# Dilated sliding attention and a soft mixture of experts on one core: 128-key tiles with halo products, four heads abreast, logits on column groups, the last weights in halves

## The chip, the cores and the metric

The kernel runs on one core of a Trainium2 chip. A core has a matrix engine (TensorE, PE in the profile, with its weight loads listed apart as PEld), a vector engine (DVE), a scalar engine (ACT), a general engine (POOL, which here only issues DMAs) and a queue engine (SP); 16 DMA engines move data between main memory and the on-chip memory (SBUF). Matrix products land in a small accumulator memory, PSUM, of eight banks of 512 fp32 values per partition. Each engine runs its own instructions in order and waits for others by semaphores. The metric is the device time of one execution in microseconds; the time of a kernel is the median of its runs.

## The reference

There are two stages. For 8 batches, 8 heads, 576 positions and a head width of 64:

```
scores = q @ k.T / 8
plain heads (0-3): keep 0 <= i-j < 32
dilated heads (4-7): keep 0 <= i-j < 128 and (i-j) % 4 == 0
attn = softmax(scores) @ v
x = attn with the heads side by side      # 4608 rows of 512
```

Then a soft mixture of 8 experts with 4 slots each, over all 4608 rows:

```
logits = x @ phi                          # 4608 x 32
d = softmax of logits over the rows;  slot_input = d.T @ x
slot_out[e] = relu(slot_input[e] @ w1[e]) @ w2[e]
out = softmax of logits over the slots @ slot_out
```

All inputs are fp32 in main memory (q, k and v are 9.4 MB each, w1 and w2 16.8 MB each), and so is the output (9.4 MB).

## The kernel before

Every load is a POOL DMA that turns fp32 into fp16 on the way. The program is written as a loop over b (10 passes: 8 batches and two to drain), each with six steps kt; the framework that builds the kernel then orders each engine's instructions by their dependencies, so the instructions of neighbouring steps are interleaved on an engine.

**Attention of one batch.** q and k of a batch arrive as `raw` tiles (L145), and DVE transposes them in 32x32 blocks: the plain heads in one instruction each (`qk_plain`, L200), the dilated heads in two parts (`qk_dil`, L209), sorted by position modulo 4 so that a dilated head becomes four plain windows of 144 positions, called residues. A head occupies 32 partitions, its width of 64 being two halves `tt`. The plain heads work in six tiles of 96 queries against 128 keys, the 32 keys ahead of a tile being part of it; this is why v is copied in a shifted form (`shift_v_plain` L184, `shift_v_left` L180). The dilated heads work in four residues of 128 queries, and 16 queries are left over in each. `emit_scores` (L238) computes a step: two heads at a time (`pair`), each on its own 32 rows of the array and in its own PSUM bank. ACT takes the exponent (L251), DVE multiplies by the mask (L256). `emit_av` multiplies by v with a column of ones (so the row sums come along), eleven products a batch (L273, L291, L304), and DVE divides (L314 reciprocal, L315 multiply). v takes three DMAs a batch: the plain heads (L157), the dilated heads (`vsa`, L163, spread by ACT at L174) and the left-over (`vsb`, L166). v tiles exist three times, raw tiles twice.

**Slots.** One batch later x is transposed by PE (L330, L342) and copied by ACT (L335, L345, L348), the logits are computed with phi repeated four times so that all 128 partitions hold the same 32 rows four times (L360, two instructions groups of 288 columns each), and ACT writes exp(logits) to `ET` (L363). Two batches later ET is transposed (`ep`, L374 to L384), masked to `er` (L391) and used for the slot sums `u` (L405), which DVE adds to `UT` (L411).

**Experts and output.** After the loop: slot inputs (L543 to L549), `hps` against w1 (L563), row sums `rs` (L572), relu (L580, L581), transposes (L584), `so` against w2 (L597), copies to `so_sb` (L604, L605), then 36 blocks of 128 output rows: one matmul (L613), one scaled copy on ACT or DVE (L616, L618), one POOL DMA (L621).

**Order of loads.** POOL issues q, k, one w1 (two in b = 3) at step kt 1 of each pass and v at kt 3, two batches ahead; in passes 6 and 7 it issues the last w1 and the eight w2, some into q/k and v tiles that have come free (L193). The lines in the code that say so:

```
for _ in range((1, 1, 1, 2, 1, 1)[b]):
    load_w1(next_w1.pop(0))
...
if b + 2 < B:
    load_v(b + 2)
```

Of the kernel before, what the change touches and what calls it, by code (L numbers as in the profile page):

```python
# [15 lines left out]
B = 8  # L16
H = 8
S = 576
# [14 lines left out]
QT = 96  # L33
NT = S // QT
SUB = S // DIL
VW = 72
LEFT = SUB - 128
NLEFT = 5 * LEFT
WP = NT // 2 * QT
NE = NT + DIL + 1  # L40
NFIN = N_ROWS // 128


def make_masks():

    a = np.arange(128)[:, None]
    i = np.arange(QT)[None, :]
    rel = 32 + i - a
    plain = (rel >= 0) & (rel < WINDOW)
    c = np.arange(LEFT)[None, :]  # L50
    rel = 32 + c - a
    left = (rel >= 0) & (rel < WINDOW) & (a < 48)
    i = np.arange(128)[None, :]
    rel = i - a
    dil = (rel >= 0) & (rel < WINDOW)
    m = [plain] * 3 + [left] * 5 + [dil] * 4
    ok = ((np.arange(128)[:, None] % 32) < LEFT) & np.ones((1, N_SLOTS), bool)
    m.append(ok)
    return np.ascontiguousarray(np.concatenate(m, axis=1).astype(np.float16))
# [3 lines left out]
def kernel(  # L63
# [12 lines left out]
    mask_np = make_masks()  # L76
    masks_dram = nc.inline_tensor(mask_np, name="masks_d")
    ident_dram = nc.inline_tensor(np.eye(128, dtype=np.float16), name="ident_d")
# [3 lines left out]
    masks = consts.tile([128, mask_np.shape[1]], FP16, name="masks")  # L82
    mask_p = masks[:, 0 : WP + NLEFT]
    mask_d = masks[:, WP + NLEFT : WP + NLEFT + 512]
    ident = consts.tile([128, 128], FP16, name="ident")
# [3 lines left out]
    emask = consts.tile([128, NE, N_SLOTS], FP16, name="emask")  # L89
    ET = consts.tile([128, N_ROWS + 64], FP16, name="ET")  # L90
# [3 lines left out]
    rrow = consts.tile([128, NFIN], FP32, name="rrow")  # L94
    so_sb = consts.tile([128, DMODEL], FP16, name="so_sb")
# [4 lines left out]
    w2t = {e: w2a_pool.tile([128, 8, DMODEL], FP16, name=f"w2_{e}", tag=f"w2_{e}") for e in range(2)}  # L100
# [4 lines left out]
    QK_SLAB, V_SLAB = 2 * (32 + S + S + 80 + S + S + 16), 4096  # L105
    kTp, kTd, qTp, qTd, vP, vD, vL = [], [], [], [], [], [], []
    for i in range(2):
        slab = fix.tile([128, QK_SLAB], FP16, name=f"qk{i}", tag=f"qk{i}")
        o = 0
        for dst, n in ((kTp, 32 + S), (kTd, S + 80), (qTp, S), (qTd, S + 16)):  # L110
            dst.append(slab[:, o : o + 2 * n].rearrange("p (s t) -> p s t", t=2))
            o += 2 * n
    for i in range(NV):
        slab = fix.tile([128, V_SLAB], FP16, name=f"v{i}", tag=f"v{i}")
        o = 0
        for dst, n in ((vP, NT), (vD, DIL), (vL, DIL)):
            dst.append(slab[:, o : o + n * 4 * VW].rearrange("p (h n d) -> p h n d", h=4, n=n))
            o += n * 4 * VW

# [6 lines left out]
    p_pool = tc.alloc_tile_pool(name="pp", bufs=4)  # L126
# [5 lines left out]
    psum_s = tc.alloc_tile_pool(name="psum_s", bufs=2, space=bass.MemoryType.PSUM)  # L132
# [22 lines left out]
    def load_v(b):  # L155
        vt = vP[b % NV]
        nc.gpsimd.dma_start(  # L157
            out=vt[32:128, :, :, 0:D], in_=v[b, 0:4].rearrange("h (t a) d -> a (h t) d", t=NT)
        )
        sa = vs_pool.tile([128, 4, DIL * D], FP16, name=f"vsa_{b}", tag="vsa")  # L160
        sb = vs_pool.tile([128, 4, DIL * D], FP16, name=f"vsb_{b}", tag="vsb")
        vstage[b] = (sa, sb)
        nc.gpsimd.dma_start(  # L163
            out=sa, in_=v[b, 4:8, 0:512, :].rearrange("h (a r) d -> a h (r d)", r=DIL)
        )
        nc.gpsimd.dma_start(  # L166
            out=sb[32 : 32 + LEFT],
            in_=v[b, 4:8, 512:576, :].rearrange("h (a r) d -> a h (r d)", r=DIL),
        )

    def spread_v_dil(b):
        sa, sb = vstage.pop(b)
        for st, dst, p0, n in ((sa, vD[b % NV], 0, 128), (sb, vL[b % NV], 32, LEFT)):
            nc.scalar.copy(  # L174
                out=dst[p0 : p0 + n, :, :, 0:D],
                in_=st[p0 : p0 + n].rearrange("a h (r d) -> a h r d", r=DIL),
            )

    def shift_v_left(b):
        nc.vector.tensor_copy(out=vL[b % NV][0:32, :, :, 0:D], in_=vD[b % NV][96:128, :, :, 0:D])  # L180

    def shift_v_plain(b):
        vt = vP[b % NV]
        nc.vector.tensor_copy(out=vt[0:32, :, 1:NT, 0:D], in_=vt[96:128, :, 0 : NT - 1, 0:D])  # L184

# [3 lines left out]
    def load_w2(e, pieces=1):  # L189
        n = 8 // pieces  # L190
        src = moe_w2[e].rearrange("(c p) f -> p c f", p=128)
        for i in range(pieces):
            nc.gpsimd.dma_start(out=w2t[e][:, n * i : n * i + n, :], in_=src[:, n * i : n * i + n, :])  # L193


    def qk_plain(ti, b):
        src = raw[(ti, b)][:, 0, :].bitcast(U32).rearrange("p (j m) -> p j m", m=32)
        t = qTp[b % 2] if ti == 0 else kTp[b % 2][:, 32 : 32 + S, :]
# [15 lines left out]
    def emit_scores(b, kt):  # L214
        kp, kd, qp, qd = kTp[b % 2], kTd[b % 2], qTp[b % 2], qTd[b % 2]
        sps = psum_s.tile([128, 2, 512], FP32, name=f"s_{b}_{kt}", tag="s")
        jobs = []
        if kt < 4:
            pair, half = kt % 2, kt // 2
            for i in range(3):  # L220
                t = 3 * half + i
                jobs.append((kp, QT * t, qp, QT * t, QT * i, QT))
            n = WP
            if half == 1:
                for r in range(DIL):
                    w = LEFT if r < 3 else 2 * LEFT
                    jobs.append((kd, SUB * r + 96, qd, SUB * r + 128, WP + LEFT * r, w))
                n = WP + NLEFT
        else:
            pair = kt - 4  # L230
            for r in range(DIL):
                jobs.append((kd, SUB * r, qd, SUB * r, 128 * r, 128))
            n = 512
        for kt_, k0, qt_, q0, c0, w in jobs:
            for tt in range(2):
                for hh in range(2):
                    p0 = 32 * (2 * pair + hh)
                    nc.tensor.matmul(  # L238
                        sps[:, hh, c0 : c0 + w],
                        kt_[p0 : p0 + 32, k0 : k0 + 128, tt],  # L240
                        qt_[p0 : p0 + 32, q0 : q0 + w, tt],
# [3 lines left out]
        return sps, n  # L245

    def emit_exp(b, kt, sps, n):
        tag, w = (("pa", WP), ("pb", WP + NLEFT), ("pd", 512))[kt // 2]
        pt = p_pool.tile([128, 2, w], FP16, name=f"{tag}_{b}_{kt}", tag=tag)
        ptile[(b, kt)] = (pt, n)  # L250
        nc.scalar.activation(out=pt[:, :, 0:n], in_=sps[:, :, 0:n], func=AF.Exp, scale=SCALE)  # L251

    def emit_mask(b, kt):
        pt, n = ptile[(b, kt)]
        m = (mask_p if kt < 4 else mask_d)[:, 0:n]
        nc.vector.tensor_tensor(  # L256
            out=pt[:, :, 0:n],
            in0=pt[:, :, 0:n],
            in1=m[:, None, :].broadcast_to([128, 2, n]),
# [4 lines left out]
    xp_t, xd_t = {}, {}  # L264

    def emit_av(b, tl):
        o = psum_o.tile([128, 4, D + 1], FP32, name=f"o_{b}_{tl}", tag="o")
        if tl < NT:
            half, i = divmod(tl, 3)
            nq = QT if (half == 0 and i == 2) else 128  # L270
            for h in range(4):
                pt, _ = ptile[(b, 2 * half + h // 2)]
                nc.tensor.matmul(  # L273
                    o[0:nq, h, :],
                    pt[:, h % 2, QT * i : QT * i + nq],
                    vP[b % NV][:, h, tl, 0 : D + 1],
                    start=(h == 0),
                    stop=(h == 3),
                    skip_group_check=True,
                )  # L280
            if b not in xp_t:
                xp_t[b] = x_pool.tile([128, NT, 4 * D], FP16, name=f"xp_{b}", tag="xp")
            dst, nq = xp_t[b][0:QT, tl, :], QT
        else:
            r = tl - NT
            if b not in xd_t:
                xd_t[b] = x_pool.tile([128, DIL + 1, 4 * D], FP16, name=f"xd_{b}", tag="xd")
            if r < DIL:
                for h in range(4):
                    pt, _ = ptile[(b, 4 + h // 2)]  # L290
                    nc.tensor.matmul(  # L291
                        o[:, h, :],
                        pt[:, h % 2, 128 * r : 128 * r + 128],
                        vD[b % NV][:, h, r, 0 : D + 1],
                        start=(h == 0),
                        stop=(h == 3),
                        skip_group_check=True,
                    )
            else:
                for r in range(DIL):  # L300
                    for h in range(4):
                        pt, _ = ptile[(b, 2 + h // 2)]
                        c0 = WP + LEFT * r
                        nc.tensor.matmul(  # L304
                            o[32 * r : 32 * r + 32, h, :],
                            pt[0:48, h % 2, c0 : c0 + 32],
# [350 lines left out]
```

## Time and profile before

| what | us |
|---|---|
| median of 3 runs | 203.83 |
| the runs | 202.67 to 204.26 |
| span of the profiled execution | 200.8 |
| PE, DVE, ACT, POOL busy | 146.6, 132.3, 100.6, 66.9 |
| PE weight loads busy | 91.8 |

Main memory is read for 62.20 MB and written for 9.44 MB. The span runs from the first to the last instruction of the profiled execution; the time of a run is longer by what lies around it, 3.0 us by the median of the runs (the page doesn't give the profiled execution's own time). In the page's second part the span is cut into 40 slices of 5.0 us, and a digit is the busy share in tenths. PEclk is the clock of PE that the records of the profile give, in tenths; GB/s counts what the DMAs wrote. A matmul's row in the timeline has its start, its duration (which includes the time through the array, so that consecutive matmuls overlap), the engine, the line, output and inputs, shapes and a count. A weight shape of 32*128 means 32 rows of the array and 128 output rows. A wait's row has the engine and line that waited, what it waited for, and the sum, count and longest of the waits in us. In the chain of waits a row has start, duration, engine, tile and line.

### The profile page before, as it was taken

How to read it: one execution, taken by the hardware profiler on the slowest of the kernel's cores; microseconds unless marked ns; L12 is line 12 of the kernel's file. 1: busy time of each engine (PE TensorE's matmuls, PEld its weight loads, DVE VectorE, ACT ScalarE, POOL GpSimd, SP SyncE). 2: the span in 40 equal slices, each digit the busy share in tenths (PEclk: the TensorE clock that was granted, in tenths of full speed). 3: DMA queues.
4: the chain of work that ended last, by engine and by line, in shares of the span. 5: the costliest groups of instructions: out<-in, count | busy, mean ns of one | idle time of the engine just before them, and what ended most of it. 6: DMA issues, size and time to landing. Idle time of an engine off the chain costs nothing.

```text
span 200.8 us, 5070 instructions
## 1 busy us (share of the span) xinstructions
PE 146.6 (73%) x2128; PEld 91.8 (46%) x2128; DVE 132.3 (66%) x354; ACT 100.6 (50%) x150; POOL 66.9 (33%) x102
## 2 busy tenths in 40 slices
PE   0126369399889989979799998998886869758600
PEld 0115256158647746646465675675655344211000
DVE  3688697678896998597779678986632120755520
ACT  2037448384872963595386675565433020655510
POOL 7736224215215403501750003055000000598850
PEclk9999999999999999999999999955555599995555
DMA  6999999999999999999999999999999400499994
GB/s 128 182 191 192 205 211 189 209 212 187 211 210 188 214 210 203 196 212 194 204 210 189 208 207 208 207 208 208 207 207 205 70 0 0 127 407 407 410 407 124
DMA packets 46422, 40.99 MB, mean 204 GB/s; under 512 B 20672, under 2 KB 33600, under 8 KB 46400
## 3 DMA queue, kind: packets, MB, share of 16 engines
q0 software_dynamic: 46112, 40.41, 117.0%
q8 instruction: 16, 0.26, 0.5%
q1 hardware_dynamic: 288, 0.27, 0.4%
q14 instruction: 6, 0.05, 0.1%
HBM read 62.20 MB, written 9.44 MB: 357 GB/s over the span
## 4 chain that ended last, share of the span: by engine, by line
PE 41%; DMA 23%; ACT 10%; issue 10%; DVE 7%; POOL 6%; POOLq 0%; ACTq 0%
DMA v_93<-in_v_dram 10%; DMA vsa_1638<-in_v_dram 8%; DMA vsa_148<-in_v_dram 5%; PE so L597 3%; POOL out_dram L621 3%; ACT ET L363 3%; PE hps L563 3%; DVE qk_89 L200 1%; ACT v_92 L174 1%; PE lg_0_977 L360 1%; PE s_4_1993 L238 1%; PE lg_0_1329 L360 1%; PE lg_0_2031 L360 1%; PE lg_0_626 L360 1%; POOL raw_0_121 L150 1%
## 5 line engine op out<-in xcount | busy, mean ns | idle before, releaser
L238 PEld LDWEIGHTS <-qk_89 32*128 32x128 f16 x448 | 14.1, 116 | 22.3 <-DVE qk_89 L200 10.5
L238 PEld LDWEIGHTS <-qk_90 32*128 32x128 f16 x448 | 14.4, 113 | 10.3 <-issue 5.1
L621 POOL DMA_DIRECT2D out_dram<-ot_3191 x1 | 0.6, 561 | 33.4 <-ACT ot_3191 L616 33.4
L360 PEld LDWEIGHTS <-phi_61 128*128 128x128 f16 x64 | 7.6, 128 | 8.1 <-issue 3.5
L613 PEld LDWEIGHTS <-ET 128*128 128x128 f16 x36 | 3.6, 99 | 14.3 <-issue 13.0
L238 PE MATMUL s_0_178<-qk_89 32*128 32x96 f16 x12 | 0.7, 270 | 9.1 <-DVE qk_89 L200 9.1
L193 POOL DMA_DIRECT2D w_5_2337<-in_moe_w_dram x1 | 0.9, 873 | 18.0 <-PE o_0_2311 L273 18.0
L580 ACT ACTIVATE h_sb<-hps 128x512 f16<-128x512 f32 x1 | 0.6, 598 | 9.8 <-PE hps L563 9.8
L605 DVE CAST so_sb<-so 128x256 f16<-128x256 f32 x1 | 0.4, 425 | 6.8 <-ACT so_sb L604 6.8
L581 DVE TENSOR_SCALAR h_sb<-hps 128x512 f16<-128x512 f32 x1 | 0.7, 692 | 6.3 <-ACT h_sb L580 6.3
L251 ACT ACTIVATE pa_0_191<-s_0_178 128x576 f16<-128x576 f32 x1 | 0.7, 651 | 7.8 <-PE s_0_178 L238 7.8
L374 PEld LDWEIGHTS <-ET 32*128 32x128 f16 x48 | 1.9, 99 | 5.5 <-ACT ET L363 5.5
L238 PE MATMUL s_2_214<-qk_89 32*128 32x96 f16 (+2 forms) x28 | 1.1, 215 | 4.3 <-DVE qk_89 L209 3.7
L405 PEld LDWEIGHTS <-ones 96*128 96x128 f16 x48 | 4.0, 103 | 0.0
L563 PEld LDWEIGHTS <-siTm 128*32 128x32 f16 x64 | 2.1, 128 | 4.1 <-issue 2.5
L563 PE MATMUL hps<-w_0_76,siTm 128*32 128x512 f16 x8 | 3.2, 548 | 1.0 <-DVE siTm L549 1.0
L193 POOL DMA_DIRECT2D w_7_2689<-in_moe_w_dram x4 | 2.8, 707 | 3.1 <-PE o_0_2663 L273 2.9
L157 POOL DMA_DIRECT2D v_92<-in_v_dram x3 | 3.6, 1195 | 0.7 <-DMA raw_0_121<-in_q_dram 0.7
L200 DVE STREAM_TRANSPOSE qk_89<-raw_0_121 128x576 uint32<-128x576 uint32 x1 | 1.3, 1256 | 3.9 <-DMA raw_0_121<-in_q_dram 3.9
L184 DVE COPY v_93<-v_93 32x1280 f16<-32x1280 f16 x2 | 1.0, 484 | 4.2 <-DMA v_93<-in_v_dram 4.2
L157 POOL DMA_DIRECT2D v_91<-in_v_dram x3 | 3.6, 1209 | 0.0
L391 DVE TENSOR_TENSOR er_2948<-ep_2933,emask 128x352 f16<-128x352 f16 x1 | 0.3, 342 | 4.9 <-PE ep_2933 L384 4.9
(1047 smaller groups left out, 614.0 us busy)
## 6 DMA issues: line engine op xcount, KB each, us to landing
w_0_76<-in_moe_w_dram POOLq DMA_DIRECT2D x1, 1024.0 KB, 18.6
w_1_77<-in_moe_w_dram POOLq DMA_DIRECT2D x1, 1024.0 KB, 18.6
w_2_78<-in_moe_w_dram POOLq DMA_DIRECT2D x1, 1024.0 KB, 14.8
w_3_79<-in_moe_w_dram POOLq DMA_DIRECT2D x1, 1024.0 KB, 13.5
w_4_80<-in_moe_w_dram POOLq DMA_DIRECT2D x1, 1024.0 KB, 17.7
w_5_81<-in_moe_w_dram POOLq DMA_DIRECT2D x1, 1024.0 KB, 16.0
w_6_82<-in_moe_w_dram POOLq DMA_DIRECT2D x1, 1024.0 KB, 13.4
w_7_83<-in_moe_w_dram POOLq DMA_DIRECT2D x1, 1024.0 KB, 18.5
```

The source lines that it names most:

```text
L150: nc.gpsimd.dma_start(out=t[:, g, :], in_=ten[b, 4 * g : 4 * g + 4].rearrange("h (p j) d -> (h p) (j d)", j=PJ),)
L157: nc.gpsimd.dma_start(out=vt[32:128, :, :, 0:D], in_=v[b, 0:4].rearrange("h (t a) d -> a (h t) d", t=NT))
L193: nc.gpsimd.dma_start(out=w2t[e][:, n * i : n * i + n, :], in_=src[:, n * i : n * i + n, :])
L200: nc.vector.transpose(out=dst, in_=src)
L238: nc.tensor.matmul(sps[:, hh, c0 : c0 + w], kt_[p0 : p0 + 32, k0 : k0 + 128, tt], qt_[p0 : p0 + 32, q0 : q0 + w, tt], start=(tt == 0), sto ...
L360: nc.tensor.matmul(lp, phi4[:, kc].rearrange("p c s -> p (c s)"), rhs, start=(kc == 0), stop=(kc == 3))
L363: nc.scalar.activation(out=ET[:, b * S : b * S + S].rearrange("p (i r) -> p r i", r=DIL)[:, 2 * rp : 2 * rp + 2, :], in_=lp, func=AF.Exp, ...
L405: nc.tensor.matmul(up[:, c, :], l, rr, start=(i == 0), stop=(i == len(jobs) - 1), skip_group_check=True)
L563: nc.tensor.matmul(hps[32 * j : 32 * j + 32, fc, :], siTm[:, dc, e, :], w1t[e][:, dc, 512 * fc : 512 * fc + 512], start=(g == 0 and dc == ...
L597: nc.tensor.matmul(so[32 * j : 32 * j + 32, :], hTm[g][:, c, 32 * j : 32 * j + 32], w2t[4 * g + j][:, c, :], start=(g == 0 and c == 0), st ...
L613: nc.tensor.matmul(fp, ET[:, r0 : r0 + 128], so_sb, start=True, stop=True)
L621: nc.gpsimd.dma_start(out=out[r0 : r0 + 128, :], in_=ot)
```

## The change

The tiles of the attention, the scores' and the logits' layout, the loads of v, the order of the weights and the output stage are rewritten.

- **Tiles.** The plain heads take 128 keys a tile (five tiles, the last of 64) and 160 queries: 128 of its own and 32 of the next tile, the halo. The dilated residues take 128 keys and 144 queries. v needs no shifted copies; in `emit_av` each plain tile after the first adds four small products with the halo of the tile before, and the left-over adds sixteen.
- **Scores.** Three groups g of up to 480 columns a pass instead of six steps; the four heads of a kind run side by side in four PSUM banks, one such buffer instead of two of two banks. One exponent and one mask a group.
- **v loads.** Five DMAs for the plain heads, one `vsa`, and four small ones straight into `vL` in place of `vsb`.
- **Logits.** ET has 192 columns a batch instead of 576: four chunks of 128 tokens go to four groups of 32 output partitions, the last 64 tokens follow with phi repeated. One exponent a batch. `er` takes fewer transposes, and DVE makes `erd` by 32x32 blocks.
- **Weights.** One w1 a pass, the other two w1 and three w2 in pass 6, then w2 of 5, 3, 4, and at the end of pass 7 w2 of 6 and 7 by halves of their columns.
- **Output.** `so` is computed by column halves, first for experts 0 to 5, then half 0 for 6 and 7, the outputs of half 0 for five batches, then half 1. The sum over the expert groups is a matmul with `spread`. Output DMAs are 15 instead of 36.

The core of the diff, "..." where lines are left out:

```diff
-    p_pool = tc.alloc_tile_pool(name="pp", bufs=4)
+    p_pool = tc.alloc_tile_pool(name="pp", bufs=2)
...
-    psum_s = tc.alloc_tile_pool(name="psum_s", bufs=2, space=bass.MemoryType.PSUM)
+    psum_s = tc.alloc_tile_pool(name="psum_s", bufs=1, space=bass.MemoryType.PSUM)
...
     def load_v(b):
         vt = vP[b % NV]
-        nc.gpsimd.dma_start(
-            out=vt[32:128, :, :, 0:D], in_=v[b, 0:4].rearrange("h (t a) d -> a (h t) d", t=NT)
-        )
+        for t in range(NP):
+            n = min(128, S - 128 * t)
+            nc.gpsimd.dma_start(
+                out=vt[0:n, :, t, 0:D],
+                in_=v[b, 0:4, 128 * t : 128 * t + n].rearrange("h a d -> a h d"),
+            )
...
+        for h in range(4):
+            nc.gpsimd.dma_start(
+                out=vL[b % NV][0:LEFT, h, :, 0:D],
+                in_=v[b, 4 + h, 512:576, :].rearrange("(a r) d -> a r d", r=DIL),
+            )
...
+GROUPS = (
+    (("P", 0), ("P", 1), ("P", 2)),
+    (("P", 3), ("P", 4), ("L", 0), ("L", 1), ("L", 2), ("L", 3), ("D", 0)),
+    (("D", 1), ("D", 2), ("D", 3)),
+)
...
+        sps = psum_s.tile([128, 4, 512], FP32, name=f"s_{b}_{g}", tag="s")
+        for kind, i in GROUPS[g]:
...
             for tt in range(2):
-                for hh in range(2):
-                    p0 = 32 * (2 * pair + hh)
+                for h in range(4):
+                    p0 = 32 * h
                     nc.tensor.matmul(
...
+            if kind == "P" and i > 0:
+                for h in range(4):
+                    lhs = probs(b, "P", i - 1, h, 128, 32)
+                    jobs.append((slice(0, 32), lhs, vt[:, h, i - 1, 0 : D + 1], -1))
...
+        nc.scalar.copy(
+            out=xT_t[b][:, 2 + c, :].rearrange("p (i r) -> p i r", r=DIL),
+            in_=rg[:, :, 0:SUB].rearrange("p r i -> p i r"),
+        )
...
+        for kc in range(4):
+            for j in range(4):
+                nc.tensor.matmul(
+                    lp[32 * j : 32 * j + 32, m - e0 : m - e0 + 128],
+                    phi4[:, kc, 0, :],
+                    xT[:, kc, 128 * j : 128 * j + 128],
...
+        nc.scalar.activation(out=ET[:, e0 : e0 + 192], in_=lp, func=AF.Exp, scale=1.0)
...
+        nc.vector.transpose(out=erd, in_=ET[:, m : m + 128].rearrange("p (a r) -> p r a", r=DIL))
...
+            if att and g == 0:
                 if b + 2 < B:
                     load_qk(0, b + 2)
                     load_qk(1, b + 2)
+                    load_weights(1)
                 elif b == 6:
+                    load_weights(len(weights))
                 else:
...
+                    for e in (5, 3, 4):
                         load_w2(e)
...
+            if att and g == 2:
                 if b + 2 < B:
                     load_v(b + 2)
+                elif b == 7:
                     slab_weights(7, "v0", V_SLAB)
+                    for s in range(2):
+                        for e in (6, 7):
+                            load_w2(e, s)
...
+    def finish_so(s):
+        cols = slice(DH * s, DH * s + DH)
+        nc.vector.tensor_copy(out=so_part[:, cols], in_=so[s])
+        rep = ring.tile([128, DH], FP32, name=f"rep{s}", tag="ring")
+        nc.tensor.matmul(rep, spread, so_part[:, cols], start=True, stop=True)
+        nc.vector.tensor_copy(out=so_sb[:, cols], in_=rep)
...
+    NHALF = 5
+    for experts in ((0, 1, 2, 3), (4, 5)):
+        for s in range(2):
+            emit_so(s, experts)
+    for s in range(2):
+        emit_so(s, (6, 7))
+        finish_so(s)
+        for b in range(NHALF):
+            emit_batch(b, DH * s, DH * s + DH)
+    for b in range(NHALF, B):
+        emit_batch(b, 0, DMODEL)
```

`emit_so` is the matmul loop of `so` for one half of the columns, `emit_batch` computes and stores 512 rows of one batch with four matmuls on 32 rows each.

## The prediction

> **What bounds the kernel now.** I read the page's slices first, for the phases.
>
> ```profile
> PE   0126369399889989979799998998886869758600
> ...
> PEclk9999999999999999999999999955555599995555
> DMA  6999999999999999999999999999999400499994
> GB/s 128 182 191 192 205 211 189 209 212 187 211 210 188 214 210 203 196 212 194 204 210 189 208 207 208 207 208 208 207 207 205 70 0 0 127 407 407 410 407 124
> ```
>
> A slice is 5.0 us. The DMA engines are full from 5 us to about 157 (loads, at some 207 GB/s as written, fp16), idle for three slices, then full again at 407 with the 9.4 MB of output. Nothing overlaps the two; the hole between them is what the chain of work fills, asked for next:
>
> ```profile
> 66.47 1.05 ACT v_92 L174
> ...
> 82.30 16.61 DMA vsa_1638<-in_v_dram
> ...
> 153.49 0.92 PE u_2950 L405 x28
> ...
> 156.48 5.63 PE hps L563 x48
> ...
> 164.43 6.28 PE so L597 x64
> ...
> 171.62 0.38 PE f_3189 L613
> ```
>
> The last slot sum u ends at 154.4; then hps, relu, transposes, so, and the first output DMA is issued at 173.0 (33.4 us of waiting on POOL before L621), 18.6 us after u. The last lands at 198.1, 25.1 us after the first issue, and 2.7 us follow. So **the end is u's end + 18.6 + 25.1 + 2.7**.
>
> What sets u? The waits:
>
> ```profile
> ACT v_91 L174 <- DMA vsa_1638<-in_v_dram: 3.5, 1, 3.5
> ...
> POOL vsa_584 L163 <- DMA w_0_76<-in_moe_w_dram: 3.5, 1, 3.5
> ...
> POOL vsb_301 L166 <- DMA v_92<-in_v_dram: 1.2, 1, 1.2
> ```
>
> Issue plus time to landing of the vsa loads (50.04+16.1, 66.01+19.0, 82.30+16.6, 99.30+14.7) gives 66.1, 85.0, 98.9, 114.0, and the spread copy L174 follows each within 0.4 us. So up to batch 7's v at 114.0 the attention runs at the pace of the transfers: 13.9 us a batch, 18.9 where two w1 are in it. The POOL lines show a second rule: vsa_584 is POOL's 24th DMA and waits for the 16th, vsb_301 the 19th and waits for the 11th. A DMA goes out only when the eighth before it has landed.
>
> From 114.0 to 154.4, 40.4 us, no transfer is waited for. Here the windows view (columns: busy time of PE, weight loads, DVE, ACT, POOL) and the timeline show PE:
>
> ```profile
> 108.00:124.00 16.00, 14.91 (x232) 9.81 (x231) 12.30 (x38) 10.62 (x16) 1.75 (x2) 1.00 1.34 203
> 124.00:139.00 15.00, 13.84 (x244) 9.90 (x243) 12.76 (x39) 8.67 (x16) 4.84 (x7) 0.69 1.24 207
> ```
>
> ```profile
> 119.00 0.40 PE L342 MATMUL rd_0_2329<-ident,xd_2141 128*128 128x128 f16 x2
> ...
> 119.34 0.50 PE L238 MATMUL s_4_2339<-qk_89 32*128 32x128 f16 x6
> ...
> 119.77 0.39 PE L342 MATMUL rd_1_2369<-ident,xd_2141 128*128 128x128 f16 x2
> ...
> 120.09 0.71 PE L238 MATMUL s_5_2383<-qk_89 32*128 32x128 f16 x9
> ...
> 120.73 0.33 PE L304 MATMUL o_10_2256<-v_93,pb_2_1887 48*32 48x65 f16 x8
> ```
>
> Nine score matmuls take 0.71 with the last one's 0.30 in it: a pair of heads each 0.105 us for 128 columns, 1.2 columns a ns. Likewise 0.107 a transpose, 0.054 a 65-column AV matmul (o_8 at 118.59, o_9 four later at 118.78, a little under it), 0.24 a logits matmul (four in 1.13), 0.027 a u matmul. Between unlike shapes something is lost: 119.34 less 119.00 is 0.34 for two transposes worth 0.21; 119.34 to 119.77 is 0.43 for three pairs worth 0.32; about **0.12 a change of shape**. So per batch: scores 4.1, AV 2.5, transposes 2.0, logits 1.9, ep 0.4, u 0.8, together 11.7, and some 21 changes 2.6: 14.3 of the 15 to 16 us. PE sets this stretch, DVE (12 to 13) is next.
>
> PEclk's 9s before 126 us do not fit: so's matmuls move 512 columns in 0.216 us (2.4 a ns), twice the rate seen at 119. I go by the spacing. On this the Trainium skill (TensorE: Matmul & The Clock Gate, "What's actually happening") says the array runs at half clock by default and at full clock after about 3.4 us of busy time. By that rule the attention runs at half clock now, as the spacing shows.
>
> **The change, part by part.**
>
> *Scores.* 13 pieces of 1344 columns, four heads abreast, two halves: 1344 x 2 / 1.2 = 2.3 us, if four row groups run together as two do. If not, 4.5. I take 2.3: hps's four matmuls, on column groups, start within 0.01 us of each other. Saved 1.8.
>
> *AV.* P: 20 mains and 16 halos at 0.054, 1.9; D 0.9; L twice 16 at 0.013 (o_10's spacing), 0.4: 3.2, 0.7 more. Each of the four P halos has 32 output rows, so two changes of shape each, 8 x 0.12 = 1.0; below that, 0 if the halo doesn't count as a change.
>
> *Logits.* Sixteen of 128 columns, four abreast: 4 x 0.107, plus 4 x 0.053 for the tail, 0.64: saved 1.3, or 0 if not abreast. *ep, transposes, u*: 0.1 less together. Score runs fall from 6 to 3: 6 changes less, 0.7.
>
> PE: 14.3 - 1.8 + 0.7 + 1.0 - 1.3 - 0.1 - 0.7 = **12.1** a batch; with the 1.4 of other stalls 13.5, against 15.5. Ends: 11.1 (halos change no shape) and 15.6 (nothing runs four abreast).
>
> *DVE.* Masks cover 5376 columns for 4672 in half as many instructions: even (2.9). Both v shifts go, 0.85 together; one AV tile less, 0.45; the new 128x128 transpose adds 0.2. About 12.0. *ACT.* Two ET exps of 0.82 become one of 192 columns, 0.35; one spread copy of 1.04 goes. The xT copy now reads PSUM in strides; 0.65 (the plain copy) to 1.3 (L363's strided one takes 0.82 for 288 columns). ACT is at 10 of 13.5, so either is hidden. One score buffer of four banks instead of two of two: scores wait for an exp of 1.7 us (1920 columns by 1.02 for 1024), which PE fills with 2.5 us of AV and transposes per group. If this cover is gone, 3 x 1.7 = 5 us a batch.
>
> *Loads.* Up to v7 there is one w1 less: -5.1 (18.9 less 13.9), so 114.0 becomes 109. But v goes from three DMAs to ten. POOL's price: 0.52 for 64 rows (L166), 0.76 for 512 (L163): four at 0.7, 0.6, 0.76, four at 0.52, 6.2 us for 3.5 us of data (v's share of 13.9). Eight-back binds: after w1 lands, POOL still has L1, L2, L3 and q to issue, 3 x 0.52 + 0.71 + 0.45 to the first packet = 2.7 us, while 3 us of v are queued. So dry time is 0 to 1.5 us a batch; I take 0.4, and 2 us at the start, where the same ten stand ahead of q1 and k1. v7 lands at 109 + 2 + 6 x 0.4 = 113.5. The same 4.5 us move the end of all loads from 159 to 164.
>
> *u.* The rest after v7 (40.4) shrinks by 13.5/15.5 to 35.2; the last batch also has one ET exp and a shorter logits chain (150.35 to 152.4 was the second), -0.7: 34.5. **u ends at 148.0**, 6.4 earlier.
>
> *Tail.* u to so is 10.0 as before. so for experts 0 to 3 at 256 columns is 16 groups x 0.108, 4 and 5 two abreast 16 x 0.108, 6 and 7 half 8 x 0.108: 4.3 (before 6.3). Then two casts of 0.43, one matmul 0.38, hand-overs 0.3, f 0.38, four copies on two engines 0.8, hand-over 0.2: 2.9. First issue u + 17.2 = 165.2; the half loads of 6 and 7 are in at 159 (164 less one 5.1), so they are hidden; unless u ends before 145.6, when they set the first issue at 159 + 0.9 + 2.9 = 162.8. Output is the same bytes, 25.1 from first issue, plus 0.2 between halves (6.4 us of first-half data against about 6.6 to the second half's issue). Rows of 1 KB instead of 2 may cost up to a tenth of the first 5.2 MB, 1.3. End: 165.2 + 25.3 + 2.7 = 193.2. The span before is 200.8 and the median 203.8, so 3.0 lie around it: **196.2**.
>
> **Rivals.**
> - *v starves the queue (slower).* If the 6.2 us of issue are not covered, 2.7 us a batch are dry: v7 at 109 + 2 + 6 x 2.7 = 127, u at 161.7, first issue 178.9: 209.9. It decides from u = 155.6, v7 at 121, 1.7 us dry a batch. For it: eight-back, and waits at v's DMAs already. Against: the engines work off q, k and w1, 10.9 us, while POOL is idle.
> - *No shorter attention.* Coarse groups, the single score buffer and halos eat PE's gain: u at 153 to 155, first issue 170 to 172, 201 to 203.5. Without four abreast (2.2 more a batch) it comes to the same. For: PE has had 1 to 2 us of such stalls. Against: masks run a group ahead.
> - *Loads set the end.* PE better than priced: first issue 158 (no dry time) to 162.8, time 189 to 194. One way there is PE at twice the column rate: its 9.5 us of streaming halve, DVE's 12.0 sets the batch, 34.5 x 12.0/13.5 = 30.7, u at 144.2, loads bind at 162.8, 193.8. This way alone has 0.05 of the 0.15, since PE, busy as it is, does not do it between 108 and 124. By the Trainium skill's rule named above it would, if the change made PE busy without breaks.
>
> **Numbers.** Forecast (192 to 200) 0.45, loads 0.15, no shorter attention 0.2, starved 0.2. 1% (2 us) is about what can be told from no change here. Faster: 0.45 + 0.15 + a quarter of the third = 0.65; same 0.14; slower 0.21. Range 189 to 207: it leaves out most of the starved case and the very best.
>
> **What would show it.** Vsa of batch 7 landing near 113 and slices of DMA without a dent below 9; four score matmuls starting together each 0.13 us for 160 columns; PE 13 to 14 us a batch; u at 148; output beginning within 2 us of the last load's landing, so no slice of zeros. Wrong if GB/s dips at each v, if PE idles before scores on the exp, or if the first half's stores wait.

## The result and the profile after

| | before | after |
|---|---|---|
| median of 4 runs each, us | 203.82 | 212.94 |
| the runs | 202.67 to 204.26 | 212.03 to 213.97 |
| after / before, 95% interval | | 1.047 (1.041 to 1.054) |
| span of the profiled execution | 200.8 | 212.2 |
| last vsa landed | 114.0 | 126.5 |
| DVE starts to add the last u to UT | 154.4 | 153.1 |
| last load landed | 159.7 | 180.4 |
| first output DMA issued | 173.0 | 185.1 |
| last output landed | 198.1 | 210.9 |

The change made the kernel 4.7% slower, where 3.7% faster was forecast. By the times of the profiled executions, the first output is 12.1 us later, the stores take 0.7 longer, and what follows them is 1.4 shorter: together the 11.4 by which the spans differ. The medians differ by less, 9.1, because the profiled execution of the new kernel was its longest (213.97). The ratios in this document leave out an execution now and then that came out somewhat longer with the kernel unchanged, and where the profiled one was of this kind ("so behind two batches" below) its times are not listed.

The page's slices of the new kernel (a slice is 5.3 us) are to be read against those of the kernel before:

```profile
PE   0011294946957748688579479998573644889400
...
PEclk9999999975585585555555555579769695555555
DMA  6999999989979989999999999999999999099998
GB/s 135 168 123 161 175 161 211 163 126 213 184 104 209 188 111 208 195 120 206 201 116 206 204 110 200 203 197 207 208 209 205 204 198 158 0 343 396 402 414 227
```

From slice 9 to 24 the GB/s row falls to between 104 and 126 in every third slice, once a batch; in the kernel before no slice but the first is under 182 until its loads run out in slice 32. After slice 24, with only weights to load, the row is at 197 to 209. Slice 35 has no DMA at all. So there are two questions: what makes the dips, and why the stores do not begin while the last loads run.

POOL's rows in the timeline answer the first (start, duration, line, output and input, count, and in brackets the idle time ahead and what ended it):

```profile
93.80 0.77 POOL L208 DMA_DIRECT2D w<-in_moe_w_dram  x1
94.53 3.62 POOL L186 DMA_DIRECT2D v<-in_v_dram  x5
99.48 0.75 POOL L192 DMA_DIRECT2D vsa<-in_v_dram  x1 [1.33 <-ACT ET L369]
102.22 0.52 POOL L196 DMA_DIRECT2D v<-in_v_dram  x1 [1.99 <-DMA raw<-in_k_dram]
107.14 1.54 POOL L196 DMA_DIRECT2D v<-in_v_dram  x3 [4.40 <-DMA v<-in_v_dram]
108.69 0.72 POOL L172 DMA_DIRECT2D raw<-in_q_dram  x1
109.39 0.73 POOL L172 DMA_DIRECT2D raw<-in_k_dram  x1
```

The w1 issued at 93.80 lands at 106.57, and only then, 0.57 later, does POOL issue the second of the four small vL loads. It is the eighth DMA after that w1. Three vL loads go out one after the other, and q follows at 108.69. What was queued by then is used up when the first vL lands at 109.98. From there to k's landing at 118.23 are 8.25 us, for three vL (0.5), q (2.9) and k (2.8): 2 us are lost. The windows view shows the loss as a rate (the last column is GB/s): it falls from 108.5 on and is back at its full value only 2.8 us after q's issue.

```profile
108.00:108.50 0.50, 0.50 (x31) 0.39 (x19) 0.50 (x2) 0.00 (x0) 0.49 (x2) 0.50 1.48 187
...
109.50:110.00 0.50, 0.50 (x19) 0.28 (x8) 0.50 (x4) 0.15 (x1) 0.50 (x1) 0.50 0.24 13
110.00:110.50 0.50, 0.40 (x8) 0.24 (x5) 0.47 (x3) 0.50 (x1) 0.50 (x2) 0.50 1.05 65
...
111.50:112.00 0.50, 0.50 (x8) 0.50 (x7) 0.21 (x1) 0.50 (x1) 0.50 (x2) 0.50 1.06 203
```

The same order stands in every pass, with 1 to 2 us lost in this stretch, and w1 lands at 40.6, 56.1, 72.9, 90.3, 106.6 and 123.2, every 16.5 us on average, where the kernel before took 13.9 in most of its batches with one w1 (15.1 in the last). The issue view (KB each, median us from issue to landing) has the price of a small load:

```profile
v<-in_v_dram POOLq DMA_DIRECT2D x32, 8.0 KB, 3.3
```

A load of 8 KB lands 3.3 us after its issue, though such loads land 0.17 us apart when several are queued. The time from an issue to its data is what the queue must cover. On this the Trainium skill (DMA: Bandwidth & Descriptors, "Anatomy of one DMA — SWDGE (gpsimd) path") gives a fixed part of about 2.0 us for each DMA, and its "Rules for kernel authors" say to join small transfers into one. The trace comes near that figure: the least time of a v load is 2.1 us, and the median of 3.3 holds the landing of loads queued ahead as well. The run with one load in place of four, below, agrees with the rule.

The second question is answered by PE's rows at the end of the loads:

```profile
175.71 1.86 PE L601 MATMUL so<-w,hTm 128*32 128x256 f16 x15 [2.99 <-DMA w<-in_moe_w_dram]
177.81 0.37 PE L601 MATMUL so<-w,hTm 128*32 128x256 f16 x1 [0.23 <-DMA w<-in_moe_w_dram]
180.44 1.86 PE L601 MATMUL so<-w,hTm 128*32 128x256 f16 x15 [2.26 <-DMA w<-in_moe_w_dram]
182.24 0.39 PE L613 MATMUL rep<-so_part,cst 128*128 128x256 f16 x1
182.82 0.37 PE L613 MATMUL rep<-so_part,cst 128*128 128x256 f16 x1 [0.19 <-DVE so_part L611]
```

The first row finishes half 0 of `so`. Its cast on DVE begins at 177.61. But next on PE stand 16 matmuls of half 1, which wait for the last two half loads (177.76, 180.40). Half 0's `rep` is issued behind them at 182.24. The framework put half 1's products ahead, and so the first output goes out 4.7 us after the last load, and the halves overlap nothing.

### The profile page after: what moved, and what is told of

Its sections match the earlier page's. It is cut to its first block, busy times and chain, and to the rows that moved or that the text cites. A ratio compares the mean times of both kernels' runs of the same rounds, so it can differ in the third digit from the quotient of the medians.

```text
span 212.2 us, 5445 instructions
## 1 busy us (share of the span) xinstructions
PE 127.7 (60%) x2342; PEld 84.2 (40%) x2342; DVE 127.3 (60%) x318; ACT 84.4 (40%) x103; POOL 90.0 (42%) x136
## 4 chain that ended last, share of the span: by engine, by line
DMA 60%; DVE 13%; POOL 9%; PE 8%; issue 3%; ACT 3%; POOLq 0%
DMA w<-in_moe_w_dram 31%; DMA raw<-in_k_dram 16%; DMA v<-in_v_dram 6%; DMA raw<-in_q_dram 6%; POOL v L196 4%; DVE qk L220 3%; PE f L620 3%; ACT om L629 3%; DVE qk L229 2%; POOL raw L172 2%; DVE p L264 2%; DVE xd L313 1%; PE o_D L299 1%; POOL w L208 1%; DVE xp L313 1%
## 5 line engine op out<-in xcount | busy, mean ns | idle before, releaser
L259 ACT ACTIVATE p<-s 128x1728 f16<-128x1728 f32 (+1 forms) x24 | 39.9, 1662 | 27.4 <-PE s L246 25.2
L299 PEld LDWEIGHTS <-p 128*128 128x128 f16 (+2 forms) x672 | 29.1, 118 | 41.3 <-DVE xp L313 15.1
L246 PE MATMUL s<-qk 32*128 32x160 f16 (+3 forms) x832 | 26.5, 263 | 20.8 <-ACT p L259 10.4
L196 POOL DMA_DIRECT2D v<-in_v_dram x32 | 16.3, 510 | 46.8 <-DMA raw<-in_k_dram 14.6
L220 DVE STREAM_TRANSPOSE qk<-raw 128x576 uint32<-128x576 uint32 x16 | 20.0, 1252 | 23.2 <-DMA raw<-in_q_dram 19.9
L299 PE MATMUL o_P<-v,p 128*128 128x65 f16 (+1 forms) x288 | 25.5, 236 | 7.6 <-DVE p L264 3.7
L186 POOL DMA_DIRECT2D v<-in_v_dram x40 | 29.0, 777 | 1.3 <-DMA raw<-in_q_dram 1.3
L264 DVE TENSOR_TENSOR p<-p,cst 128x1728 f16<-128x1728 f16 (+1 forms) x24 | 25.7, 1072 | 3.5 <-ACT p L259 3.5
L246 PEld LDWEIGHTS <-qk 32*128 32x128 f16 x832 | 16.5, 115 | 24.9 <-issue 12.0
L229 DVE STREAM_TRANSPOSE qk<-raw 128x320 uint32<-128x320 uint32 (+1 forms) x32 | 20.1, 655 | 0.1
L313 DVE TENSOR_TENSOR xp<-o_P,rc_P 128x256 f16<-128x256 f32 x40 | 16.3, 420 | 0.7
L213 POOL DMA_DIRECT2D w<-in_moe_w_dram x10 | 8.8, 918 | 15.1 <-DMA w<-in_moe_w_dram 8.6
## 6 DMA issues: line engine op xcount, KB each, us to landing
v<-in_v_dram POOLq DMA_DIRECT2D x32, 64.0 KB, 12.1
```

The source lines that it names most:

```text
L186: nc.gpsimd.dma_start(out=vt[0:n, :, t, 0:D], in_=v[b, 0:4, 128 * t : 128 * t + n].rearrange("h a d -> a h d"),)
L196: nc.gpsimd.dma_start(out=vL[b % NV][0:LEFT, h, :, 0:D], in_=v[b, 4 + h, 512:576, :].rearrange("(a r) d -> a r d", r=DIL),)
L220: nc.vector.transpose(out=dst, in_=src)
L229: nc.vector.transpose(out=o, in_=i)
L246: nc.tensor.matmul(sps[:, h, c0 : c0 + w], kt[p0 : p0 + 32, k0 : k0 + 128, tt], qt[p0 : p0 + 32, k0 : k0 + w, tt], start=(tt == 0), stop=( ...
L259: nc.scalar.activation(out=pt, in_=sps[:, :, 0:n], func=AF.Exp, scale=SCALE)
```

## The experiments

All medians come with the ratio to the kernel before and its 95% interval. "UT" is when DVE starts to add the last u; the other columns are landings and the first output's issue in the profiled execution. The sections below explain the names of the runs.

| run | us | ratio | last vsa | UT | loads end | first output |
|---|---|---|---|---|---|---|
| w1 behind v | 214.77 | 1.052 (1.047 to 1.057) | 122.0 | 154.9 | 181.1 | 185.8 |
| seven v DMAs | 202.67 | 0.993 (0.988 to 0.998) | 115.4 | 156.3 | 167.9 | 174.4 |
| before, with ten v DMAs | 211.57 | 1.039 (1.034 to 1.045) | 130.8 | 160.3 | 179.9 | 182.8 |
| so behind two batches | 211.07 | 1.035 (1.031 to 1.039) | - | - | - | - |
| w1 behind v, so behind two | 212.05 | 1.040 (1.037 to 1.044) | 121.6 | 156.4 | 180.6 | 180.1 |
| late copy of v | 213.45 | 1.048 (1.043 to 1.054) | 125.1 | 155.4 | 179.3 | 184.0 |
| seven, late copy | 201.31 | 0.988 (0.984 to 0.993) | 114.2 | 147.6 | 167.7 | 172.0 |
| seven, late copy, so behind five | 199.42 | 0.979 (0.973 to 0.984) | 113.8 | 147.2 | 166.6 | 169.5 |
| so behind five | 211.18 | 1.037 (1.032 to 1.042) | 126.4 | 154.0 | 180.4 | 180.3 |
| seven, late copy, so behind three | 199.28 | 0.979 (0.975 to 0.983) | 114.6 | 148.1 | 167.6 | 169.7 |
| the same behind five, w2 whole | 201.38 | 0.989 (0.986 to 0.993) | 113.9 | 149.4 | 166.2 | 171.5 |

### The number of v DMAs

**In the kernel before.** Nothing of the new tiles, groups or end; only the three v DMAs are made ten: the plain heads one by one, as shown, `vsa` in two halves and `vsb` by head in the same way.

```diff
-        nc.gpsimd.dma_start(
-            out=vt[32:128, :, :, 0:D], in_=v[b, 0:4].rearrange("h (t a) d -> a (h t) d", t=NT)
-        )
+        for h in range(4):
+            nc.gpsimd.dma_start(
+                out=vt[32:128, h, :, 0:D], in_=v[b, h].rearrange("(t a) d -> a t d", t=NT)
+            )
...
```

> The kernel before with one edit: its three v DMAs of a batch are split into ten (v by head in four, vsa in two, vsb by head in four), same bytes, same tiles, same order behind w1. Theory (eight loads in flight, and 2.8 us from an issue to its first data): as in the new kernel, the eighth of v goes out only when w1 has landed and q two issues later, so a batch of loads takes 15.5 to 17 us instead of 13.9, vsa of the last batch lands at 122 to 130 instead of 114.0, u ends 4 to 14 us later, and the time is 208 to 219 us. Rival (the new kernel's own tiles, group sizes or orders make it slow, not the number of v DMAs): 202 to 206 us.

Measured 211.57 us: this edit alone costs 3.9%, nearly as much as the whole change. POOL's rows and its longest wait for a DMA are those of the new kernel:

```profile
98.04 0.79 POOL L191 DMA_DIRECT2D w<-in_moe_w_dram  x1
...
106.41 0.52 POOL L170 DMA_DIRECT2D vsb<-in_v_dram  x1 [3.20 <-DMA raw<-in_k_dram]
111.33 1.46 POOL L170 DMA_DIRECT2D vsb<-in_v_dram  x3 [4.40 <-DMA w<-in_moe_w_dram]
113.04 0.74 POOL L145 DMA_DIRECT2D raw<-in_q_dram  x1 [0.25 <-issue]
```

```profile
POOL vsb L170 <- DMA w<-in_moe_w_dram: 27.7, 6, 5.2
```

The wait's sum of 27.7 us over six passes is named outright here: the small load waits for w1 (landed 111.06). The last vsa is at 130.8, 16.8 later than in the kernel before and a little past the expected range. Here the small loads read rows of 1 KB, in the new kernel rows of 256 bytes, and both lose the time: short rows of the small loads are not the cause.

The traces show one thing more about the rule of eight. POOL's loads signal eight semaphores (the counters by which a landing is told) in turn, so the eighth before is the last load on the same semaphore, in both kernels. Whether the chip sets the limit or the program as it was built, no run shows.

**In the new kernel, seven.** vL comes by one DMA into a staging tile and ACT spreads it.

```diff
-        for h in range(4):
-            nc.gpsimd.dma_start(
-                out=vL[b % NV][0:LEFT, h, :, 0:D],
-                in_=v[b, 4 + h, 512:576, :].rearrange("(a r) d -> a r d", r=DIL),
-            )
+        nc.gpsimd.dma_start(
+            out=sb[0:LEFT], in_=v[b, 4:8, 512:576, :].rearrange("h (a r) d -> a h (r d)", r=DIL)
+        )
...
+        nc.scalar.copy(
+            out=vL[b % NV][0:LEFT, :, :, 0:D],
+            in_=sb[0:LEFT].rearrange("a h (r d) -> a h r d", r=DIL),
+        )
```

> The new kernel with vL loaded by one DMA into a staging tile (rows of 1 KB) and spread by one more ACT copy: seven v DMAs a batch instead of ten, the order unchanged. Theory (eight loads in flight): with seven behind it, the next q is the eighth behind w1 and goes out when w1 lands, with all of v still to come, some 2.9 us against the 2 us that q takes to start; the dry time falls from 2.6 us to 0 to 0.7 us a batch, loads end at 162 to 168, time 193 to 201 us. Rival (a cost per DMA, in proportion to their number): three of the seven added ones are gone, so 3/7 of the 17 us, loads end at about 172 to 175, time 204 to 208 us.

Measured 202.67 us, between the two ranges. The loads end at 167.9, where the theory had them; that the time is 1.7 us above its range has another reason, which comes below. The runs spread from 201.0 to 204.2, and the profiled one, at 203.88, is among the longer. q is now the eighth behind w1 and goes out as soon as w1 has landed (97.00):

```profile
91.77 0.52 POOL L196 DMA_DIRECT2D vsb<-in_v_dram  x1 [2.10 <-ACT xT L334]
97.53 0.71 POOL L172 DMA_DIRECT2D raw<-in_q_dram  x1 [5.24 <-DMA v<-in_v_dram]
98.24 0.71 POOL L172 DMA_DIRECT2D raw<-in_k_dram  x1
98.95 0.75 POOL L211 DMA_DIRECT2D w<-in_moe_w_dram  x1
```

From vsb's landing (100.52) to k's (106.23) are 5.71 us, exactly the data of q and k: the gap is gone. A batch of loads takes 15.0 us. Against the 13.9 of the kernel before 1 us remains, here between k's landing and w1's (5.9 us for 5.0 us of data). Two passes of the kernel before show the same 5.7 to 5.9; the cause stays open.

**w1 behind v.** The order of issue instead of the number.

```diff
                     load_qk(1, b + 2)
-                    load_weights(1)
...
                     load_v(b + 2)
+                    load_weights(1)
```

> The new kernel with one edit: the w1 load of each batch pass is issued behind that pass's ten v loads instead of ahead of them. Same loads, same bytes, same ten v transfers. Theory (queue dry behind w1: the second vL load goes out only once w1 has landed, with 2.9 us of data left and q still four issues away): the dips of the GB/s row at v go, vsa of the last batch lands at 109 to 115 instead of 126.5, all loads end at 162 to 167 instead of 180.4, and the time falls to 193 to 200 us. Rival A (the v transfers are slow in themselves, by their 256-byte rows) and rival B (buffers come free too late, so that loads wait for the arithmetic): the order of issue changes nothing, loads end at 178 to 182, time 210 to 214 us.

Measured 214.77 us: the theory failed, and a batch of loads takes 17.0 us. By the numbers alone its rivals would do. Against short rows speaks the kernel before with ten, whose small loads have rows of 1 KB; against buffers that come free late, that at the dips POOL waits for loads and not for arithmetic. The number of DMAs was the cause, and not where w1 stands among them. The rows show why the order did not help:

```profile
102.76 1.54 POOL L196 DMA_DIRECT2D v<-in_v_dram  x3 [2.20 <-DMA v<-in_v_dram]
104.28 0.77 POOL L208 DMA_DIRECT2D w<-in_moe_w_dram  x1
```

The three small loads now wait until k has landed (102.18), take 1.5 us to issue, and w1 goes out behind them at 104.28 with 1.9 us of data left (the last vL lands at 106.13). w1 lands at 113.17 with 5.0 us of data, so by the landings its data begin at about 108.1: 2 us are lost again. Four loads that together carry 0.7 us of data hold four of the eight places, wherever they stand. That reading comes from the rows; no run tried it by itself.

### What the late loads hold up

With seven v DMAs the last vsa landed 11 us earlier, and yet u came 3 us later than in the new kernel. ACT's rows of that run:

```profile
105.40 1.61 ACT L262 ACTIVATE p<-s 128x1728 f16<-128x1728 f32 x1
115.46 1.04 ACT L202 COPY v<-vsa 128x1024 f16<-128x1024 f16 x1 [8.45 <-DMA vsa<-in_v_dram]
116.41 1.04 ACT L205 COPY v<-vsb 16x1024 f16<-16x1024 f16 x1
117.35 1.59 ACT L262 ACTIVATE p<-s 128x1728 f16<-128x1728 f32 x1
```

The exp at 117.35 is the last of batch 5. It needs nothing of the v that is copied ahead of it, which is batch 7's; the framework ordered it so. Seven exps were left when that v landed; in the new kernel the same copy stood one pass later, and only four were left. Hence the 40.9 us (156.3 less 115.4) after the last vsa there, against 26.6 (153.1 less 126.5). So the copy was put behind the first exp of its own pass (`ex`; `issue_after` sets only the order on the engine).

```diff
+            if att and g == 0 and b > 0:
+                with tc.issue_after(ex.ins):
+                    spread_v_dil(b)
...
-            if att and g == 1 and b + 1 < B:
-                spread_v_dil(b + 1)
```

With ten DMAs:

> The new kernel with the ACT copy of v out of its staging tile moved: for batch b it stands behind the first exp of pass b, where the new kernel issues it before the last exp of pass b-1. Ten v DMAs, w1 and the end unchanged. Theory now: the copy holds the exps behind it in ACT's order until v has landed (37.8 us of waiting for vsa), so the arithmetic of a pass cannot run ahead of the v of the next; without it u ends at 140 to 150 instead of 153.4, but the loads still come 16.5 us a batch, end at 178 to 182 and set the end: 210 to 214 us. Rival (the copy's wait is the main cause, and the loads are late because buffers come free late behind it): loads end before 172 and the time is under 206 us.

Measured 213.45 us, within the range, with the loads ending at 179.3: the copy's wait is not what makes the loads late. But u came at 155.4, not at 140 to 150. By the rows the next wait in order took the place, DVE's transposes of the next batch's q and k, with the divisions behind them; no run moved these transposes.

```profile
113.06 1.25 DVE L220 STREAM_TRANSPOSE qk<-raw 128x576 uint32<-128x576 uint32 x1 [2.63 <-DMA raw<-in_q_dram]
116.82 1.26 DVE L220 STREAM_TRANSPOSE qk<-raw 128x576 uint32<-128x576 uint32 x1 [0.68 <-DMA raw<-in_k_dram]
...
119.60 0.18 DVE L312 RECIPROCAL rc_D<-o_D 128x4 f32<-128x4 f32 x1 [0.17 <-PE o_D L299]
```

With seven:

> Seven v DMAs a batch, and the copy of v behind the first exp of its own pass. With seven alone the last vsa landed at 115.4 and u yet ended at 156.3, with the copy of v ahead of the exps of a pass that does not need it. Theory (ACT's order holds the attention): u ends at 138 to 148, the loads' end (167 to 169) and the order of so in the end set the first output at 171 to 174: 199 to 202 us. Rival (PE at half clock is the bound of the attention, with or without the wait): u at 153 to 157, time 202 to 204 us.

Measured 201.31 us, u at 147.6: 33.4 us after the last vsa, where the kernel before takes 40.4 after a last vsa at the same time. About as much work is left at that time, 6 of 24 exps here and 10 of 48 there. So the new arithmetic gains some 7 us once the loads and the copy do not hold it. It moves the total by little (1.4 us against seven DMAs alone), because now the last loads (167.7) and the order on PE set the first output at 172.0. The time is within the expected range.

### The end

> The new kernel with one edit in its end: the 16 matmuls of so's second half for experts 6 and 7 are queued on PE behind the f matmuls of the first two batches of half 0; loads untouched. Theory (PE's written order holds half 0's rep and f behind half 1's so, which waits for the last load): so of half 0 is complete at 177.6, its rep follows at once, the first output goes out at 180 to 182 instead of 185.1, and half 1's so lies beside the stores of half 0 (6.6 us): time 208 to 210 us. Rival (the stores would wait for the last loads on the DMA engines anyway, or half 1 comes too late and leaves a gap of its own): 212 to 214 us.

```diff
-    for s in range(2):
-        emit_so(s, (6, 7))
...
+    emit_so(0, (6, 7))
+    finish_so(0)
+    for b in range(2):
+        emit_batch(b, 0, DH)
+    with tc.issue_after(last_f[0].ins):
+        emit_so(1, (6, 7))
+    for b in range(2, NHALF):
+        emit_batch(b, 0, DH)
+    finish_so(1)
...
```

Measured 211.07 us, 1 to 3 us short of the expectation's gain: half 0's third batch stood behind the wait for the last load (in the next run, which has the same end, the second output is issued at 180.97 and the third at 184.32). Together with w1 behind v:

> Both edits together: w1 behind v, and so's second half for experts 6 and 7 behind two batches of half 0. If the two causes add up: the first edit's 13 to 19 us and up to 4 us more, less what the first already takes from the second, since PE rather than the last load then sets half 0: 190 to 197 us. If the second edit only matters while the loads end last, this equals the first edit's time within 1 us.

Measured 212.05 us, outside both expectations. As the first edit gained nothing, this says no more than the run above. Behind all five batches:

> The new kernel, ten v DMAs, with so's second half for experts 6 and 7 queued on PE behind all five batches of half 0 (behind two of them gave 211.07 us, with a stall of 3.3 us between the second and the third output, in which PE waited for the last load). Theory (the order on PE, not the DMA engines, holds half 0): the first output goes out before or at the end of the loads, no stall in half 0: 207.5 to 210 us. Rival (stores beside the last loads gain nothing): 211 us or more.

```profile
175.11 1.87 PE L601 MATMUL so<-w,hTm 128*32 128x256 f16 x15 [2.24 <-DMA w<-in_moe_w_dram]
177.49 0.37 PE L613 MATMUL rep<-so_part,cst 128*128 128x256 f16 x1 [0.52 <-DVE so_part L611]
178.37 0.40 PE L621 MATMUL f<-so_sb,ET 32*128 32x256 f16 x4 [0.52 <-DVE so_sb L614]
...
183.44 1.89 PE L601 MATMUL so<-w,hTm 128*32 128x256 f16 x16
185.85 0.37 PE L613 MATMUL rep<-so_part,cst 128*128 128x256 f16 x1 [0.52 <-DVE so_part L611]
```

Measured 211.18 us, again less gain than expected; by the time alone the rival (211 or more) would stand. The rows decide for the mechanism: the first output goes out at 180.33, with the last load, instead of 4.7 us behind it. But half 1's chain (so, cast, rep, copy, f) now begins only after half 0's last f, its first output is issued at 188.58, and half 0's stores have landed at 189.11; the next data land at 191.95, where stores otherwise follow each other by 1.3. So about 1.5 us go back.

With seven DMAs and the late copy:

> As the run before it, and so's second half for experts 6 and 7 queued on PE behind all five batches of half 0. Theory: half 0 is complete with the third half load from the end (about 165.3), the first output goes out 4.4 us later at 169 to 171, half 1 follows without a gap: 196 to 199 us. Rival (PE at half clock sets half 0): first output at 172 to 175, no gain over the run before it, 200 to 204 us.

Measured 199.42 us, 0.4 above the range, with the first output at 169.5 as expected, 2.5 us ahead of the run without this edit. The same with half 1 behind three batches:

> As the kernel with seven v DMAs, the late copy and the reordered end (199.42 us), but so's second half for experts 6 and 7 stands behind three batches of half 0 instead of five. There the loads had ended at 166.6, before the first output, and half 1's first output came 4.0 us after half 0's last, a gap in the stores of about 1 us. Theory: the gap goes, 198 to 199 us. Rival (half 0's later batches are held up by the 1.9 us of so as much as half 1 gains): 199 to 200 us.

Measured 199.28 us: no difference, as the rival had it. The gap moved into half 0 (its third output is issued at 171.34, the fourth at 173.92). And with the last two w2 whole:

```diff
-                    for s in range(2):
-                        for e in (6, 7):
-                            load_w2(e, s)
+                    for e in (6, 7):
+                        load_w2(e)
```

> As the kernel with seven v DMAs, the late copy and the reordered end (199.42 us), but w2 of experts 6 and 7 loaded whole, two DMAs of 1 MB in place of four of 0.5 MB. Theory (the column halves earn what half 0 gains on the last load, once PE's order lets it): the first output waits for the last load, 166 to 166.6, and the 31 matmuls behind it, and goes out at 170.5 to 172 instead of 169.5: 200.5 to 202 us. Rival (the halves earn nothing, or cost by their smaller rows): 198.5 to 199.7 us.

Measured 201.38 us, as the theory had it: the column halves earn 2 us once PE's order lets them.

The version at 199.3 to 199.4 us beats both kernels, the one before by 2.1%.

## Why the prediction was wrong

- **The dry time.** The step that failed is "dry time is 0 to 1.5 us a batch; I take 0.4". The rule of eight, POOL's price for each issue (L1, L2, L3 and q from 107.14 to 109.40) and their order were right. Mis-sized was what lies around them: the sum left out the 0.57 from w1's landing to L1's issue, and "0.45 to the first packet" let q's data flow at the full rate at once. The full rate is back at 111.5, 4.9 us after w1's landing where 2.7 were counted, and the 3 us of queued v do not cover that. "2 us at the start" was too small as well: vsa of batch 2 landed at 43.7 against 38.3. So v7 is 109 plus 5.5 at the start plus 12 over five batches, 126.5 instead of 113.5, and the loads end at 180.4 instead of 164. The rival "v starves the queue" had the mechanism, the price (2.7; measured 16.5 less 13.9, 2.6) and v7 (127), with a chance of 0.2.
- **What the late loads do.** The rival carried them through u (161.7, 209.9 us). That was wrong: u came at 153.1. The lateness reached the end through w2 instead, which is loaded behind all v; the prediction counted the loads' end only as a side case (164).
- **The half loads.** "Hidden" was wrong for two reasons: the loads end 16 us later, and PE's order is not the written one. From the landing of half 0's last load (175.66) the prediction's 3.8 us would have given 179.5; the order made it 185.1. The 3.8 was too short too: with the order put right, 5.3 us pass (175.06 to 180.33, so behind five). Of that `so` for experts 6 and 7 takes 1.9 us (15 matmuls in 1.87) where 0.9 was counted: the granted clock is 0.50 there; in the run "seven, late copy", where it is 1.00, 15 of them take 1.03.
- **PE.** The 12.1 us a batch were about right. The windows view of the new kernel has 11.5, 11.2, 11.2 and 11.5 us of busy PE in four batches and 12.2 in the fifth (columns: busy PE, weight loads, DVE, ACT, POOL):

```profile
108.00:124.50 16.50, 12.19 (x245) 8.62 (x233) 12.37 (x31) 8.19 (x9) 8.45 (x14) 0.50 1.21 175
```

Four heads do run abreast (24 score matmuls of 144 columns in 0.91, 0.12 for four as priced). Once the loads are back at the old pace and the copy is out of the way, 33.4 us pass from the last vsa to u, where 34.5 were forecast, and u is at 147.6, where 148.0 was. DVE, the single score buffer and the halos did not eat it, in that run.
- **The end.** From first issue to last landing 25.8 us (forecast 25.3), then 1.3 (2.7). Around the span lie 1.8 us in every run of the new kernel; with the same 1.8, an estimate, the profiled execution of the kernel before took 202.6, one of its shorter ones, and the prediction's 3.0 set its span against the median of all.
- **The sum.** With the three causes taken out (ten v DMAs, the early copy, the order on PE) the kernel takes 199.4 us, still 3.2 above the forecast. There the loads set the first output, which the prediction held for a side case: the last load of half 0 lands at 163.9, not 159, and 5.6 us later, not 3.8, the first output goes out, at 169.5 instead of 165.2.

## What to carry to other kernels

Where the issuing engine may have only so many DMAs under way, price a split in places and not in bytes: ask which DMA waits for the long one's landing, and whether the data queued then last until the next large load has been issued and has started (here nearly 3 us from its issue to the full rate, plus 0.5 for each small issue ahead of it). An in-order engine that waits early for the next batch's load (ACT's copy, DVE's transposes) ties this batch's work to the load. Pieces of a last load only help if the consumer's order on its engine, as it is built and not as it is written, lets the first piece through.

## What was not expected of the hardware

The granted clock of PE did not set the time while the loads were late: two executions of the new kernel with mean clocks of 0.704 and 0.850 took 212.03 and 212.30 us. The profiled execution of the new kernel had 0.679 and a span of 212.2 us, that of w1 behind v, with the same arithmetic, 0.812 and 213.4. The kernel before with ten v DMAs had 0.959, with 9s in its clock row up to slice 36, and a span 8.8 us longer than the kernel before at 0.874.
